# Batches on partition halves, Q and x transposed by DMA, and a new order of loads in a fused attention and MLP kernel

## The chip, the cores and the metric

The kernel runs on one core of one Trainium2 chip. The metric is the device time of one execution in microseconds (us). The kernel before takes 316.9 us (median). Times in profiles are measured from the start of the profiled execution's span, which is 1.7 to 3 us shorter than the metric. "Landing" is the time from the issue of a transfer to its arrival. TensorE is called PE, VectorE DVE, ScalarE ACT, GpSimd POOL and SyncE SP, as in the profile.

## The reference

Eight batches, eight heads, 576 tokens, 64 features a head. Attention is linear: no softmax, KV is a 64x64 matrix per head. Every output row is divided by its root mean square and multiplied by a gain, the heads are laid side by side to 4608 rows of 512, and an MLP with ELU follows.

```python
kv  = einsum('bhsd,bhse->bhde', k, v)
out = einsum('bhsd,bhde->bhse', q, kv)
out = out / sqrt(mean(out*out, -1) + 1e-6) * g_norm      # per head, 64 features
x   = out.transpose(0, 2, 1, 3).reshape(4608, 512)
h   = x @ w_in                                           # 512 -> 2048
out = where(h > 0, h, exp(min(h, 0)) - 1) @ w_out        # 2048 -> 512
```

## The kernel before

Rows are worked off in nine tiles of 512: tiles 0 to 7 are the first 512 rows of each batch, tile 8 collects the last 64 rows of all eight. While PE multiplies tile T by w_in ("first layer", eight steps of 8 products) and tile T-1 by w_out ("second layer", eight halves of 8 products), the attention of tile T+1 is slipped in between. PE needs Q and x with features on partitions, so PE itself transposes both, through PSUM (the buffers that PE's products are written to), and DVE and ACT copy the results out. The parts that matter:

```python
def q_t():                                   # Q of tile T, on PE
    qt_ps = at_tile(BF16).rearrange("p (r t) -> p r t", r=NPAIR)
    for p in range(NPAIR):
        q_t_mm(bf["q", T], qt_ps, p)         # 16 transposes in all
    nc.vector.tensor_copy(out=qT[:, 0:2, :], in_=qt_ps[:, 0:2, :])
    nc.scalar.copy(qT[:, 2:4, :], qt_ps[:, 2:4, :])
# ... cut: square, sum over a head, 1/rms by Ln and Exp, scale ...
def x_t():                                   # x of tile T, on PE: 16 more
    for c in range(KC):
        for j in range(J):
            nc.tensor.transpose(xt_ps[:, c, j*P:j*P+P], xs[:, j, c*P:c*P+P], ident)
    nc.vector.tensor_scalar(out=x[:, 0:2, :], in0=xt_ps[:, 0:2, :], scalar1=g_col, ...)
    nc.scalar.mul(x[:, 2:4, :], xt_ps[:, 2:4, :], g_col)    # the gain comes for free here
# ... cut ...
for T in range(2, NT):
    second = {i: (lambda i=i: mm2_half(T - 1, i)) for i in range(8)}
    if T + 1 < NT:
        at, start = attention(T + 1), {"kv": 0, "q": 1, "se0": 2, "se1": 4, "x": 6}
        cast_all(T + 1)                      # on POOL, fp32 to bf16
    if T + 2 < B:
        fetch(T + 2)                         # on SP's queue, in order
    first_products(T, at, second, start)
```

## Time and profile before

| | before |
|---|---|
| time, median | 316.9 us |
| first product of the first layer of tile 0 | 21.84 us |
| first product of tile 1 / tile 2 | 49.0 / 77.6 us |
| one middle tile | 31.5 us |
| last product to the end | 5.9 us |

From the page of the kernel before: busy us of each engine, its share of the span and its number of instructions, then two rows of 40 time slices, in tenths (granted PE clock; mean busy share of the 16 DMA engines).

```profile
PE 295.2 (94%) x1905; PEld 149.7 (48%) x1941; DVE 179.5 (57%) x217; ACT 155.4 (50%) x217; POOL 67.1 (21%) x117
...
PEclk9999999999999999999999999999999999999998
DMA  7999959940861076108510861034101010100122
```

PE is the bottleneck, at full clock, and from tile 2 on DMA comes in bursts, one a tile, with most of the time idle.

Busy time by stretch, kernel before: for each stretch its length, then busy us and instructions of each engine, the clock, the DMA share and the rate.

```profile
core 0: us, PE busy (x) PEld busy (x) DVE busy (x) ACT busy (x) POOL busy (x), PEclk, DMA share, GB/s
21.84:49.03 27.19, 23.30 (x178) 12.92 (x181) 18.54 (x25) 15.85 (x25) 6.41 (x11) 1.00 1.02 211
49.03:77.64 28.61, 26.93 (x187) 13.86 (x188) 18.06 (x22) 18.53 (x25) 16.58 (x28) 1.00 0.63 225
...
109.74:141.26 31.52, 31.31 (x210) 16.14 (x212) 19.48 (x22) 16.07 (x22) 8.03 (x14) 1.00 0.40 142
```

In the last line, a middle tile, PE is busy 31.3 of 31.5 us: only work taken off PE can make it shorter. The two lines above it are the filling of the pipeline, and there PE does wait.

The chain of waits, kernel before: start, length, what. It shows what the 31.5 us are made of.

```profile
109.74 1.73 PE h_ps L318 x8
111.47 1.73 PE o_ps L360 x8
113.19 1.11 PE at L165 x36
...
136.92 0.89 PE at L281 x16
...
149.39 0.89 PE at L175 x16
```

Line 318 is a step of the first layer, 360 half a product of the second, 165 the KV products, 281 the transposes of x, 175 those of Q. The last two, 0.89 us each, are what the change takes off PE.

### The profile page before, as it was taken

To read this page: it belongs to the slowest core of one execution; us is meant where nothing else is said; L and a number is where in the kernel's file an instruction comes from. 1 tells how busy PE (TensorE), PEld (TensorE's weight loads), DVE (VectorE), ACT (ScalarE), POOL (GpSimd) and SP (SyncE) were. 2 spreads that over 40 slices of the span, in tenths; PEclk is the share of its full clock that TensorE was granted. 3 is DMA by queue.
4 is the path that set the end of the run, shared out by engine and by line. 5 is a ranking of instruction groups with operands and counts; after the bars stand their busy time and mean duration, and the time that the engine had idled before them with its cause. 6 is when DMAs were issued, how large, how long until landed. Compare 5 with 4: busy or idle time off the path is not lost.

```text
span 313.9 us, 4706 instructions
## 1 busy us (share of the span) xinstructions
PE 295.2 (94%) x1905; PEld 149.7 (48%) x1941; DVE 179.5 (57%) x217; ACT 155.4 (50%) x217; POOL 67.1 (21%) x117
## 2 busy tenths in 40 slices
PE   8677979999999999999999999999999999999992
PEld 4444535444554545455545554545455445444440
DVE  4565783487267646764786468646765576544300
ACT  3555954585465445544554455445543554334210
POOL 0465205870082008200720081002000000000000
PEclk9999999999999999999999999999999999999998
DMA  7999959940861076108510861034101010100122
GB/s 254 321 290 256 206 109 388 375 149 2 264 240 67 0 265 238 69 0 278 225 67 2 261 243 67 0 112 92 69 1 67 2 67 2 67 33 34 69 67 67
DMA packets 28597, 42.24 MB, mean 135 GB/s; under 512 B 5536, under 2 KB 17824, under 8 KB 28576
## 3 DMA queue, kind: packets, MB, share of 16 engines
q1 hardware_dynamic: 24352, 37.75, 34.5%
q0 software_dynamic: 4224, 4.19, 8.0%
q8 instruction: 15, 0.25, 0.3%
q14 instruction: 6, 0.05, 0.0%
HBM read 36.70 MB, written 9.44 MB: 147 GB/s over the span
## 4 chain that ended last, share of the span: by engine, by line
PE 78%; DMA 8%; DVE 5%; ACT 3%; POOL 2%; issue 2%; SPq 1%; DVEq 0%; POOLq 0%
PE o_ps L360 36%; PE h_ps L318 34%; DMA w_in_sb<-in_moe_w_in_dram 4%; DVE gT L344 2%; DMA st_k<-in_k_dram 2%; DMA st_v<-in_v_dram 2%; PE at L165 2%; PE at L281 2%; PE at L187 2%; PE at L175 2%; ACT elu_e L327 1%; DVE elu_e L336 1%; POOL v_bf L130 1%; POOL k_bf L130 1%; DVE xs L221 1%
## 5 line engine op out<-in xcount | busy, mean ns | idle before, releaser
L318 PE MATMUL h_ps<-xT,w_in_sb 128*128 128x512 bf16 (+1 forms) x564 | 133.7, 376 | 3.6 <-DMA w_in_sb<-in_moe_w_in_dram 1.7
L360 PE MATMUL o_ps<-w_out_sb,gT 128*128 128x512 bf16 x562 | 134.4, 379 | 0.8
L327 ACT ACTIVATE elu_e<-h_ps 128x1024 bf16<-128x1024 f32 (+1 forms) x74 | 74.0, 1002 | 60.6 <-PE h_ps L318 59.4
L360 PEld LDWEIGHTS <-gT 128*128 128x128 bf16 x576 | 56.3, 98 | 67.2
L336 DVE TENSOR_SCALAR elu_e<-elu_e 128x1024 bf16<-128x1024 bf16 (+1 forms) x73 | 35.3, 484 | 91.1 <-ACT elu_e L327 90.9
L318 PEld LDWEIGHTS <-w_in_sb 128*128 128x128 bf16 x584 | 55.1, 98 | 62.9 <-DMA w_in_sb<-in_moe_w_in_dram 2.4
L344 DVE TENSOR_TENSOR gT<-elu_e,h_ps 128x1024 bf16<-128x1024 bf16 (+1 forms) x66 | 79.5, 1205 | 6.9
L130 POOL CAST q_bf<-st_q 128x512 bf16<-128x512 f32 x32 | 18.9, 628 | 132.9 <-DMA st_q<-in_q_dram 110.6
L370 ACT COPY o_sb<-o_ps 128x512 f32<-128x512 f32 x36 | 21.1, 586 | 25.4 <-PE o_ps L360 25.4
L206 ACT ACTIVATE sq<-at 128x1024 bf16<-128x1024 f32 (+1 forms) x18 | 17.5, 979 | 14.8 <-PE at L187 12.2
L130 POOL CAST v_bf<-st_v 128x512 bf16<-128x512 f32 (+1 forms) x36 | 20.9, 622 | 12.2 <-DMA st_v<-in_v_dram 11.7
L130 POOL CAST k_bf<-st_k 128x512 bf16<-128x512 f32 (+1 forms) x35 | 20.7, 636 | 7.7 <-DMA st_k<-in_k_dram 7.7
L211 DVE TENSOR_REDUCE ss<-sq 128x16 f32<-128x1024 bf16 x16 | 19.5, 1218 | 4.0 <-ACT sq L206 3.8
L221 DVE TENSOR_TENSOR xs<-at,ss 128x1024 bf16<-128x1024 f32 x16 | 19.5, 1218 | 0.6 <-ACT ss L218 0.6
L291 ACT ACTIVATE xT<-at,g_col 128x1024 bf16<-128x1024 bf16 x8 | 8.9, 1114 | 19.4 <-DVE xT L288 19.4
L421 PE MATMUL idle_ps<-zeros,ident 128*128 128x512 bf16 x43 | 12.4, 422 | 1.6 <-POOL ident masks.py:199 1.4
L250 ACT COPY qT<-at 128x1024 bf16<-128x1024 bf16 x8 | 8.1, 1012 | 11.5 <-DVE qT L249 11.5
L165 PE MATMUL at<-v_bf,k_bf 64*128 64x128 bf16 x288 | 10.1, 216 | 2.8 <-DVE v_bf L130 2.0
L165 PEld LDWEIGHTS <-k_bf 64*128 64x128 bf16 x288 | 8.4, 94 | 7.0 <-issue 5.4
L187 PEld LDWEIGHTS <-qT 128*128 128x128 bf16 x128 | 8.4, 98 | 5.9 <-issue 2.5
L187 PE MATMUL at<-bd_kv,qT 128*128 128x128 bf16 x120 | 9.1, 219 | 2.2 <-DVE xs L221 2.2
L241 ACT CAST bd_kv<-at 64x256 bf16<-64x256 f32 x14 | 5.2, 369 | 9.8 <-PE at L165 9.7
(46 smaller groups left out, 107.1 us busy)
## 6 DMA issues: line engine op xcount, KB each, us to landing
st_q<-in_q_dram SPq DMA_DIRECT2D x16, 512.0 KB, 5.5
out_dram<-o_sb SPq DMA_DIRECT2D x16, 512.0 KB, 2.6
st_k<-in_k_dram SPq DMA_DIRECT2D x7, 1152.0 KB, 8.4
st_v<-in_v_dram SPq DMA_DIRECT2D x7, 1152.0 KB, 10.8
w_in_sb<-in_moe_w_in_dram POOLq DMA_DIRECT2D x4, 512.0 KB, 18.4
w_out_sb<-in_moe_w_out_dram POOLq DMA_DIRECT2D x4, 512.0 KB, 20.0
st_k<-in_k_dram SPq DMA_DIRECT2D x2, 576.0 KB, 6.8
st_v<-in_v_dram SPq DMA_DIRECT2D x2, 576.0 KB, 7.8
```

What stands on the lines that cost most here:

```text
L130: eng.tensor_copy(out=out_, in_=in_)
L165: nc.tensor.matmul(kv_ps[s][:, u * P : u * P + P], lhsT=bf["k", T][rows, j, 2 * u : 2 * u + 2, :], rhs=bf["v", T][rows, j, 2 * u : 2 * u + ...
L187: nc.tensor.matmul(ov[:, u, :, s, :], lhsT=qT[:, p, j * P : j * P + P], rhs=bd_kv[:, T, p, :], start=True, stop=True,)
L206: nc.scalar.activation(sq, se_ps, AF.Square)
L211: nc.vector.reduce_sum(out=ss, in_=sq.rearrange("p c (h e) -> p (c h) e", h=H), axis=AX.X)
L221: nc.vector.tensor_tensor(out=xs.rearrange("p c (h e) -> p (c h) e", h=H), in0=se_ps.rearrange("p c (h e) -> p (c h) e", h=H), in1=ss.to_b ...
L318: nc.tensor.matmul(h_ps[a][:, cs], lhsT=w_in_sb[:, c, f * P : f * P + P], rhs=x[:, c, cs], start=(c == 0), stop=(c == KC - 1),)
L327: nc.scalar.activation(e[:, lo:hi, :], ps, AF.Exp)
L336: nc.vector.tensor_scalar(out=e[:, lo:hi, :], in0=e[:, lo:hi, :], scalar1=1.0, scalar2=1.0, op0=ALU.min, op1=ALU.subtract,)
L344: nc.vector.tensor_tensor(out=gT[T][:, 2 * i + lo : 2 * i + hi, :], in0=e[:, lo:hi, :], in1=h, op=ALU.add if relu else ALU.max,)
L360: nc.tensor.matmul(o_ps[T, j], lhsT=gT[T][:, f, j * P : j * P + P], rhs=w_out_sb[:, f, :], start=(f == 0), stop=(f == FC - 1),)
L370: nc.scalar.copy(o_sb[T][:, j % 2, :], o_ps.pop((T, j)))
```

## The change

The intent: (a) let DMA transpose Q and x, which frees PE of 1.78 us a tile; (b) tile by "slots" of 64 rows, so that every batch lies on partition halves and the ninth tile is no longer made of leftovers; (c) make the first two tiles with features on partitions from the start, which needs no transposed x, with the mean of squares from a product with a matrix of ones; (d) load the weights first and hold batch 1 back; (e) move all later batch loads to POOL's queue. The core of the diff, cut:

```diff
-            nc.vector.tensor_copy(out=qT[:, 0:2, :], in_=qt_ps[:, 0:2, :])      # Q through PE and PSUM
-            nc.scalar.copy(qT[:, 2:4, :], qt_ps[:, 2:4, :])
+    def turn_q(b):
+        for s in range(2):
+            nc.sync.dma_start_transpose(out=qt[:, s]..., in_=bf["q", b][s*64:s*64+64]...)
...
-        def x_t():  # 16 transposes on PE, gain applied on the way out of PSUM
+                for i in (2 * h, 2 * h + 1):                      # behind each half of x
+                    nc.sync.dma_start_transpose(
+                        out=xT[T][:, :, i * P : i * P + P], in_=st["xs"][:, i, :])
+            def gain():                                           # in place, on DVE
+                nc.vector.tensor_scalar(out=xT[T][:, :, cols], in0=xT[T][:, :, cols],
+                                        scalar1=g_col, scalar2=None, op0=ALU.mult)
...
+    def fetch_all(b):
+        for name, src in (("q", q), ("k", k), ("v", v)):
+            fetch(name, src, b, eng=nc.gpsimd)
...
+    hold(w_out_sb[0:1, 3, 0:64])            # SP waits for the first quarter of w_out
+    for name, src in (("k", k), ("v", v), ("q", q)):
+        fetch(name, src, 1)
...
+    mm2_all(0, 8)                           # then casts, KV, Q, y, mean, 1/rms, x of tile 1
...
+    early = {3: ("v",), 6: ("sum0", "inv0", "mul0"), 7: ("sum1", "inv1")}     # tile 1's window
+    late = {4: ("kv",), 5: ("se0",), 6: ("se1",), 7: ("mul1",)}
...
+            early = {2: ("sum0", "inv0"), 4: ("sum1", "inv1"), 5: ("gain0",), 7: ("gain1",)}
+            late = {0: ("kv",), 1: ("se0",), 2: ("mul0",), 3: ("se1",), 4: ("mul1", "ahead")}
+        second = {i: (lambda i=i: mm2_half(T - 1, i + 2)) for i in range(6)}
+        window(T, at, early, late, second, (), "AB")
+        mm2_half(T, 0)                      # two halves of the tile's own second layer
+        mm2_half(T, 1)
```

"early" pieces enter the engines' orders before the ELU of their step, "late" ones behind it; "ahead" is cast_all of batch T+2, then its successor's loads, then turn_q.

## The prediction

> **What bounds it now.** TensorE. The engine summary shows PE busy 295 of the 313.9 us span. Cut into stages (busy time by stretch), a middle tile takes 31.5 us with PE busy 31.3, granted clock 1.00; DVE 19.5, ACT 16.1, DMA 40%. The chain of waits spells the 31.5 out: sixteen groups of 8 products at 1.73 (27.6), KV products 1.11, Q x KV 0.89, two sets of 16 PE transposes (Q, then x) at 0.89 each. The first layer starts at 21.84 us, waits again for w_in at 27.6 and 31.4 (timeline); tile 2 starts at 78.2. The last product ends near 308, so the tail is about 6.
>
> **What the change does.**
> 1. Removes both sets of transposes from PE from tile 2 on: 1.78 us a tile, all on the critical path; seven tiles, 12.5 us. Their PSUM evacuations (DVE 0.68+0.75, ACT 1.01+1.11) go too, but hide today. Tiles that cross a batch split a few products: under 0.1 us each.
> 2. Adds per tile two DMA transposes of 64x2304 bf16 and four of 128x512 on SP, about 1.1 MB, and two gain multiplies (about 0.42 each, by the 128x1024 bf16 tensor-scalar). The Trainium skill, "DMA: Bandwidth & Descriptors", section "Latency and other measured facts", gives 261 GB/s for a non-contiguous DMA transpose: an estimate of 4 to 5 us of transfer a tile, on DMA 60% idle. No trace here has one yet. From the second half of x to its gain there are about 5 us; two transposes should land in 3 to 4.
> 3. The next output halves move behind their own tile's first layer; the last ELU (ACT 1.02, DVE 0.43+1.22, plus a gain) has about 3 us of PE work to hide behind: about 0.4 us stall. So 30.1 us a middle tile, not 29.7.
> 4. Start. Weights no longer share DMA with batch 1, and x of tile 0 is made transposed, its mean by a ones matrix. From the measured 350 GB/s and cast times the first layer starts at 17 to 18 us and w_in no longer starves it: 4 to 5 us gained. Given back in part: batch 1 loads only after the first w_out quarter, about 29 us, and lands near 35 to 42, so PE waits some 5 us before the tile-1 attention (32 output products, 6.9 us, bridge part). In tile 1's window the batch-2 attention is squeezed into steps of 1.7 us with one PSUM buffer: waits of 3 us at its second Q x KV and 3 to 4 for its transposed x. Net, tile 2 starts near 80 to 81 us with 3.5 us of tile 1's second layer done: gain 1 to 2 us.
> 5. Tail: last stores per 128 rows on two queues: about 1 us.
>
> **Sum.** 12.5 - 2.5 + 1.5 + 1: about 12 us. 316.9 becomes about 305 us; 80% range 297 to 313. Chances: faster 0.80, within 2% 0.13, slower 0.07.
>
> **What would show it.** No PE transposes after tile 1; tile period 29.7 to 30.4; first-layer start before 18.5 us; idle PE between 38 and 46 us for batch 1 or w_out; idle PE near 75 to 81 before tile 2; DMA transposes landing in 2 to 4 us.
>
> **What would make it wrong.** DMA transposes landing in over 6 us: the second gain, ahead of the last ELU in DVE's order, then stalls PE by the excess, and 2 us of it a tile cancels the gain. Or in-order SP blocking stores behind transposes. The other way, batch 1 arriving earlier gives 5 us more.

## The result

The change takes 337.4 us (median of 4 runs, 332.9 to 338.3; one of them, 338.3, counts as slow and is left out of the ratio). Executions over 1.5% slower than the fastest of the same kernel are left out of the means. Ratios here are the mean time of one kernel's runs over that of the other's of the same rounds, so not quite the ratio of the quoted medians: 1.0595, interval 1.0528 to 1.0661. It is 6% slower; I had forecast 4% faster.

| start of | before | after | note |
|---|---|---|---|
| first layer, tile 0 | 21.84 | 18.66 | predicted 17 to 18 |
| tile 1 | 49.03 | 60.84 | more of the second layer of tile 0 is done by then |
| tile 2 | 77.64 | 98.44 | predicted 80 to 81 |
| tile 3 | 109.74 | 139.19 | tile 2 took 40.75 us |
| tile 4 | 141.26 | 173.29 | tile 3 took 34.10 us |
| end of span | 313.9 | 335.6 | |

The difference of 21.7 us splits from this table. Tile 2 starts 20.8 later, but with two output halves (16 products, 3.5 us) of tile 1 already done: 17.3 net. Tile 2 adds 8.7, tile 3 adds 2.6. Tiles 4 to 8 gain 5.5 and the tail 1.4.

From the page of the change, the lines that answer to those of before:

```profile
PE 296.9 (88%) x1658; PEld 136.7 (41%) x1658; DVE 176.4 (53%) x226; ACT 144.8 (43%) x203; POOL 72.2 (22%) x134
...
PEclk9999987998958997899989999999999999999999
DMA  7999989594999599129931244237132221402222
```

PE executes 247 instructions fewer and is busy just as long: the clock row shows why, it drops in the first half of the run. The DMA row is mostly full there too, up to slice 20, and quiet afterwards.

Busy time by stretch, the change (fill to tile 1, tile 1, tile 2, tile 3, tile 5):

```profile
core 0: us, PE busy (x) PEld busy (x) DVE busy (x) ACT busy (x) POOL busy (x), PEclk, DMA share, GB/s
...
18.66:60.84 42.18, 34.67 (x190) 15.63 (x188) 21.45 (x34) 24.27 (x36) 9.53 (x12) 0.92 0.97 247
60.84:98.44 37.60, 23.77 (x140) 10.90 (x140) 18.19 (x22) 16.78 (x23) 20.84 (x41) 0.87 0.88 257
98.44:139.19 40.75, 34.78 (x185) 15.57 (x186) 19.24 (x22) 13.43 (x19) 16.95 (x33) 0.87 0.78 233
139.19:173.29 34.10, 31.58 (x182) 14.79 (x180) 19.23 (x22) 13.93 (x20) 10.79 (x21) 0.95 0.66 168
...
203.65:233.77 30.12, 29.91 (x181) 14.28 (x180) 18.60 (x22) 13.93 (x20) 0.00 (x0) 1.00 0.39 73
```

Tile 5 is the change as meant: 30.1 us, what I had predicted for every middle tile. Tiles 1, 2 and 3 are long, and the share of DMA falls from 0.88 to 0.66 as they recover.

Lines picked from the timeline, the change, in tile 1's preparation, at its end and in tile 2: start, length, engine, line, instruction, and in brackets how long the engine had been idle and what ended it.

```profile
45.71 0.62 PE L452 MATMUL qt_ps<-ident,q_bf 128*128 128x128 bf16 x7 [1.08 <-DVE q_bf L97]
48.95 0.58 PE L184 MATMUL y_ps<-qT,bd_kv 128*128 128x64 bf16 x2 [0.84 <-ACT qT L95]
50.59 1.91 PE L379 MATMUL o_ps<-w_out_sb,gT 128*128 128x512 bf16 x4
54.73 1.03 PE L379 MATMUL o_ps<-w_out_sb,gT 128*128 128x512 bf16 x4
...
81.72 0.88 PE L216 MATMUL at<-bd_kv,qT 128*128 128x128 bf16 x8 [3.75 <-DVE xs L275]
98.44 3.59 PE L358 MATMUL h_ps<-xT,w_in_sb 128*128 128x512 bf16 x8 [9.20 <-DVE xT L288]
...
115.45 9.99 SPq L282 DMA_TRANSPOSE xT<-xs  x4
115.95 0.75 POOL L87 DMA_DIRECT2D st_q<-in_q_dram  x1
116.69 0.75 POOL L87 DMA_DIRECT2D st_k<-in_k_dram  x1
117.43 0.75 POOL L87 DMA_DIRECT2D st_v<-in_v_dram  x1
129.10 0.49 DVE L288 TENSOR_SCALAR xT<-xT,g_col 128x1024 bf16<-128x1024 bf16 x1 [6.70 <-DMA xT<-xs]
130.02 1.22 DVE L335 TENSOR_TENSOR gT<-elu_e,h_ps 128x1024 bf16<-128x1024 bf16 x1
131.29 3.57 PE L358 MATMUL h_ps<-xT,w_in_sb 128*128 128x512 bf16 x8 [5.97 <-DVE gT L335]
```

Three things are to be read here, besides the waits of 3.75 and 9.20 us in tile 1's window. First, four output products take 1.91 us at 50.6 and four of the same size 1.03 at 54.7: PE runs at half clock for a while after a stretch of small waits. Second, at 115.5 SP issues the transposes of x, and half a microsecond later POOL issues the loads of a whole batch; the gain on DVE then waits 6.7 us for x, the ELU stands behind the gain on DVE, and PE waits 6.0 us for the ELU to free its PSUM. Third, after that wait 8 products take 3.57 us instead of 1.73. The Trainium skill, "TensorE: Matmul & The Clock Gate", Part 1, says that the array starts out at half clock, is released by activity and falls back after an idle window of about 3.4 us; it puts products of 512 columns at 426.7 ns cold and 215.7 ns warm. This trace agrees with the two rates (1.73 us / 8 = 216 ns warm; the 12 products of zeros at the very start take 5.30 us, about 440 ns each, although the clock column gives 1.00 there). It also shows a drop at 47.8 us with no single wait above 1.1 us; in the 3.41 us before it PE was busy for 1.48.

All x transposes of the change, and all Q transposes from batch 2 on (the view of one source line, its last line each, 282 then 307):

```profile
DMA to landing us min/median/max: 2.3/2.4/12.4
...
DMA to landing us min/median/max: 4.0/4.6/10.3
```

Alone an x transpose lands in 2.4 us, as predicted; beside loads it took up to 12.4.

### The profile page after: what moved, and what is told of

Read it like the earlier page. It is cut to its first block, busy times and chain, and to the rows that moved or that the text cites. A ratio compares the mean times of both kernels' runs of the same rounds, so it can differ in the third digit from the quotient of the medians.

```text
span 335.6 us, 4283 instructions
## 1 busy us (share of the span) xinstructions
PE 296.9 (88%) x1658; PEld 136.7 (41%) x1658; DVE 176.4 (53%) x226; ACT 144.8 (43%) x203; POOL 72.2 (22%) x134
## 3 DMA queue, kind: packets, MB, share of 16 engines
q0 software_dynamic: 9184, 25.43, 26.5%
## 4 chain that ended last, share of the span: by engine, by line
PE 68%; DVE 11%; DMA 8%; ACT 8%; issue 3%; SPq 0%; POOL 0%; DVEq 0%; POOLq 0%
PE o_ps L379 31%; PE h_ps L358 29%; DMA xT<-xs 8%; DVE gT L335 4%; ACT elu_e L318 3%; PE at L156 2%; PE idle_ps L448 2%; DVE elu_e L327 2%; PE at L216 1%; DVE xT L288 1%; ACT rT L203 1%; ACT rT L204 1%; ACT elu_h L322 1%; DVE xs L275 1%; PE qt_ps L452 1%
## 5 line engine op out<-in xcount | busy, mean ns | idle before, releaser
L358 PE MATMUL h_ps<-xT,w_in_sb 128*128 128x512 bf16 (+1 forms) x580 | 140.4, 389 | 20.9 <-DVE gT L335 10.6
L379 PE MATMUL o_ps<-w_out_sb,gT 128*128 128x512 bf16 x576 | 138.7, 387 | 1.9 <-DVE gT L335 1.2
L335 DVE TENSOR_TENSOR gT<-elu_e,h_ps 128x1024 bf16<-128x1024 bf16 (+1 forms) x68 | 82.0, 1205 | 7.1
L391 ACT COPY o_sb<-o_ps 128x512 f32<-128x512 f32 x32 | 18.7, 585 | 35.8 <-PE o_ps L379 33.0
L97 POOL CAST q_bf<-st_q 128x384 bf16<-128x384 f32 (+2 forms) x33 | 17.4, 573 | 53.8 <-DMA qT<-q_bf 32.8
L97 POOL CAST k_bf<-st_k 128x384 bf16<-128x384 f32 (+2 forms) x33 | 17.3, 568 | 16.6 <-PE at L156 13.4
L288 DVE TENSOR_SCALAR xT<-xT,g_col 128x1024 bf16<-128x1024 bf16 x14 | 7.0, 499 | 17.5 <-DMA xT<-xs 17.5
L97 POOL CAST v_bf<-st_v 128x384 bf16<-128x384 f32 (+1 forms) x31 | 15.7, 548 | 1.7 <-DMA st_v<-in_v_dram 1.7
L253 ACT ACTIVATE sq<-at 128x1024 bf16<-128x1024 f32 x14 | 14.4, 1028 | 2.3 <-PE at L216 2.2
L448 PE MATMUL idle_ps<-zeros,ident 128*128 128x512 bf16 x24 | 8.4, 506 | 1.4 <-POOL ident masks.py:199 1.4
L207 DVE SCALAR_TENSOR_TENSOR xT<-y_ps,g_col,rT 128x512 bf16<-128x512 f32 x6 | 4.5, 749 | 6.5 <-ACT rT L204 4.7
```

The lines of the kernel that those rows point to most:

```text
L97: eng.tensor_copy(out=out_, in_=in_)
L335: nc.vector.tensor_tensor(out=gT[T][:, 2 * i + lo : 2 * i + hi, :], in0=e[:, lo:hi, :], in1=h, op=ALU.add if relu else ALU.max,)
L358: nc.tensor.matmul(h_ps[a][:, cols], lhsT=w_in_sb[:, c, f * P : f * P + P], rhs=xT[T][:, c, cols], start=(c == 0), stop=(c == KC - 1 and l ...
L379: nc.tensor.matmul(o_ps[T, j], lhsT=gT[T][:, f, j * P : j * P + P], rhs=w_out_sb[:, f, :], start=(f == 0), stop=(f == FC - 1),)
L391: nc.scalar.copy(o_sb[T][:, j % 2, :], o_ps.pop((T, j)))
L448: nc.tensor.matmul(ps[:, 0, :], lhsT=ident, rhs=zeros, start=True, stop=True)
```

## The experiments

Thirteen kernels ran after the change. They are grouped by question. Tile lengths are the distances between first products of neighbouring tiles, as the chain of waits gives them (the timeline puts a product that follows a busy PE up to 0.2 us earlier).

### Do the loads slow the transposes, or does something else? (e1, e2, e5)

**e1_fetch_later**: loads of batches 4 to 7 wait for x.

```diff
+    def gated_fetch(T, b):
+        nc.gpsimd.tensor_copy(out=after_x, in_=xT[T][0:1, 3, 496:512])   # waits for transpose and gain
+        fetch_all(b)
-                    if b + 1 < B:
-                        fetch_all(b + 1)
+        gated_fetch(T + 1, T + 3)           # behind the window of tile T
```

> Edit: the loads of batches 4 to 7 are issued only after the x of the tile in hand has been transposed and scaled (GpSimd first reads a few elements of it). Theory A (the loads share the 16 DMA engines with the x transposes, which then take 7 to 12 us instead of 2.4): no x transpose lands later than about 4 us, the waits of 9.2 us before tile 2, 6.0 in tile 2 and about 3 in tile 3 shrink to under 3, 0.5 and 0.5, the slow clock after them goes too, tiles 2 and 3 fall from 40.8 and 34.1 us to about 30.2; total 337 to 312-318 us. Rival B (DMA transposes are slow when issued behind each other on the one in-order queue, whatever the loads do): landings stay at 7 to 12 us and the total stays within 4 us of 337.

Measured: 324.6 us (ratio to before 1.0256, 1.0229 to 1.0282). The slowest x transpose landed in 3.8 us. Tile 2 started at 94.5 instead of 98.4 (its wait 4.9 instead of 9.2 us) and took 35.5 us; tile 3 took 30.1. So theory A held for x and rival B fell, but the total missed the forecast's upper end by 7 us: the wait before tile 2 stayed above the 3 us that I had expected, tile 2 began at half clock after it, and the loads that had been let go now met the Q transposes of the next batch. The timeline of this run:

```profile
92.74 3.55 SPq L307 DMA_TRANSPOSE qT<-q_bf  x2
...
95.01 0.75 POOL L87 DMA_DIRECT2D st_q<-in_q_dram  x1 [0.32 <-POOL after_x L628]
...
107.93 0.35 PE L225 MATMUL at<-bd_kv,qT 128*64 128x128 bf16 x5 [2.24 <-DMA qT<-q_bf]
```

Q was issued at 92.7 and PE still waited for it at 107.9; the slowest Q transpose took 13.8 us. (In the next expectation I put PE's wait there at 7.9 us; that was ACT's wait for PE, PE itself waited 2.24.)

**e2_gain_later**: loads as in the change, the gains moved.

```diff
-            early = {2: ("sum0", "inv0"), 4: ("sum1", "inv1"), 5: ("gain0",), 7: ("gain1",)}
+            early = {2: ("sum0", "inv0"), 4: ("sum1", "inv1")}
         mm2_half(T, 0)
         mm2_half(T, 1)
+        at["gain0"]()
+        at["gain1"]()
```

> Edit: loads as in the change; only the two in-place gains move, from steps 5 and 7 of the first layer to behind the two output halves that follow it. If what costs the time is that the first gain stands ahead of the ELU in VectorE's order (theory C: order, not the transfers), the stalls in tiles 2 and 3 shrink although the x transposes still land in 7 to 12 us: tile 2 from 40.8 to about 33, tile 3 from 34.1 to about 30.5, total about 326. If the transfer itself is the limit (A), the stall only moves behind the gain to the next tile's first product, tile 2 stays above 37, total above 333. Also the 1 us stall at the end of each quiet tile should fall to under 0.5.

Measured: 326.7 us (ratio 1.0338, 1.0281 to 1.0395). The slowest x transpose still took 12.1 us, yet tile 2 fell to 33.5 us and tile 3 to 30.2, and PE waited only 0.9 us, at the next tile's first product, where it had waited 6.0:

```profile
131.52 1.90 PE L358 MATMUL h_ps<-xT,w_in_sb 128*128 128x512 bf16 x8 [0.90 <-DVE xT L288]
```

This is theory C, to the number. So the two causes are needed together in tiles 2 and 3: the loads made the transposes slow, and the place of the gain, ahead of the ELU in DVE's order, made PE pay for it. Either cure alone gives most of the loss there back. Before tile 2 the wait stayed at 8.4 us, since there the gain feeds PE directly. (My hope for the end of a tile came to nothing: quiet tiles still took 30.2.)

**e5_gate_all**: the loads wait for x and for Q, and the gains stand late.

```diff
+        nc.gpsimd.tensor_copy(out=after_x, in_=xT[T][0:1, 3, 496:512])
+        nc.gpsimd.tensor_copy(out=after_x, in_=qT[bq][0:1, 1, 1, 8, 0:16])
+        fetch_all(b)
```

> Edit: the loads of batches 4 to 7 wait for both kinds of transposes (x of the next tile and Q of the batch after), and the gains stand behind the two output halves. In the run with only the x transposes protected, those landed in 2.4 to 3.8 us but the Q transposes of batch 3 then took 13.8 us beside the loads that had been let go, and tile 2 waited 7.9 us for them. If contention is the cause for both kinds, no transpose after tile 1 lands later than 6 us, tiles 2 to 7 all take 29.6 to 30.2 us, total 312 to 316: all that the contention costs, with the fill as slow as before. If something else delays the Q transposes, tile 2 stays above 35 us and the total above 320.

Measured: 322.4 us (ratio 1.0189, 1.0144 to 1.0235, unclear), above the 312 to 316 that I expected. From the end of tile 1's window on no transpose landed later than 5.0 us, as expected; within that window the Q transposes of batch 2, which the load of batch 3 still met, took up to 10.3. By stretch (tile 1, tile 2, tile 3):

```profile
61.72:95.00 33.28, 23.78 (x141) 10.96 (x140) 17.95 (x22) 16.80 (x23) 11.64 (x22) 0.92 0.62 175
95.00:127.75 32.75, 32.56 (x185) 14.83 (x185) 19.49 (x22) 13.61 (x20) 11.09 (x23) 0.93 0.65 173
127.75:157.90 30.15, 29.96 (x180) 14.18 (x181) 18.73 (x22) 13.95 (x21) 10.93 (x23) 1.00 0.74 192
```

From tile 3 on, all is as planned. Tile 2 has no waits left but runs at a clock of 0.93, because tile 1 ends with waits of 3.7 us (second Q x KV) and 4.9 us (x). Contention and the place of the gain account for 15 us here (337.4 to 322.4); the rest of the loss lies before tile 2, and the contention inside tile 1's window is still in it.

### What does the slow clock cost, and what do transposes on PE cost? (e4, e3)

**e4_warm**: products of zeros in the waits.

```diff
+    idle(40, at_tile())                     # before tile 2
+            if i == 7 and T in (2, 3):
+                idle({2: 26, 3: 14}[T], at_tile())
```

> Edit: nothing but products of zeros, 40, 26 and 14 of them, put where TensorE waits for x before tile 2, in tile 2 and in tile 3; the waits stay, the clock should not drop. After each of these waits 8 products took 3.57 us instead of 1.73 and the next ones were partly slow, about 2.7 us a time. If the slow clock after a wait is a cost of its own, total falls by 4 to 8 us and the mean clock rises from 0.95 to 0.97-0.98; if it is not, the total stays at 337 or rises by what the added products overrun (0 to 2 us).

Measured: 332.1 us, 5.2 less than the change, with the mean clock up from 0.953 to 0.984. The waits stayed. So about 5 us of the loss was half clock after the waits, and not the waits themselves. The total alone would be thin evidence, since one of the runs of the change took 332.9 us; but that run had a mean clock of only 0.956, and the profile of e4 has the gain where the zeros are: tile 2 took 35.8 us instead of 40.75 and tile 3 32.8 instead of 34.1.

**e3_x_on_pe**: x of tiles 2 to 8 is transposed on PE again (the x_t piece of the kernel before, at step 5), Q stays on DMA.

> Edit: x of tiles 2 to 8 is transposed on TensorE again, as in the kernel before; Q stays on DMA, all else as in the change. It prices the one part. If DMA transposes of x are what the change loses by (A): quiet tiles cost 30.1 + 0.9 - up to 0.5 = 30.5 to 31.0, but tiles 2 and 3 fall to about 31 too and the wait before tile 2 from 9 to 2-3 us; total 315 to 321. If the fill of the pipeline (until the first product of tile 1 at 60.8 us) is the larger loss, it stays above 325.

Measured: 321.6 us (ratio 1.0159, 1.0141 to 1.0177), just outside the upper end of 315 to 321. A quiet tile took 30.8 us. The change without DMA transposes of x beats the change by 16 us, but not the kernel before: that points at the fill again.

### What holds the start of tile 1? (s1, s2, s3, s4)

From the first KV product of batch 1 to the first product of tile 1 the change takes 18.25 us (42.59 to 60.84). I compare that stretch.

**s1_no_hold**: the hold is removed, batch 1 loads right behind batch 0.

> Edit, on the change: batch 1 loads right behind batch 0 instead of behind the first quarter of w_out. My prediction held that TensorE would wait for the late batch 1. In the profile k, v and q of batch 1 land near 34.7, 37.7 and 40.7 us, before TensorE is through with the 32 output products at 42.6. Theory chain: what holds tile 1 is the serial chain of casts, copies, squares, means and scalings behind it, so with an early batch 1 the first product of tile 1 stays within 2 us of 60.8. Theory load: it comes 4 to 6 us earlier. Either way the first layer of tile 0 should now wait for w_in again, 1 to 5 us.

Measured: 18.2 us (46.44 to 64.62). The first layer of tile 0 now waits for w_in, so all of it lies 3.8 us later. My predicted wait for batch 1 does not exist.

**s2_no_inv**: without logarithm and exponential in tile 1 (wrong; relative error of 0.26).

```diff
+    for rt in r:
+        nc.gpsimd.memset(rt, 1.0)
     def inv_of(c, ps):
-        inv_t(r[c // 2][:, c % 2, :], ps)
+        pass
```

> Edit, on the change, wrong on purpose: the logarithm and exponential of tile 1 (8 ScalarE calls of 128x512, 0.6 to 0.7 us each) are left out, the factor is set to one. If the serial chain on ScalarE and VectorE holds tile 1 (chain), its first product comes 3 to 6 us earlier than 60.8. If TensorE's own work or the loads of w_out hold it, it moves by under 1 us.

Measured: 18.1 us (42.79 to 60.91). It is not ACT's Ln and Exp.

**s3_warm_tile1**: 17 products of zeros in PE's waits.

> Edit, on the change: 17 products of zeros in the waits of TensorE between 44.9 and 50 us, in tile 1's serial stretch, nothing else. Two theories fell here (late loads; ScalarE's logarithm and exponential). What the profile still shows between 47 and 54.5 us is TensorE nearly always busy at half clock: groups of 4 output products take 1.7 to 1.9 us instead of 0.9. If that is what holds tile 1, its first product comes at 58 to 59.5 us instead of 60.8 and the groups from 50.6 on take 0.9. If it still comes at 60.3 or later, the stretch is held by VectorE and ScalarE in a way that no single part shows, and it stays open.

Measured: 17.45 us (44.10 to 61.55). The clock was now full, the groups of four output products took 0.87 us apart, and still only 0.8 us was won (the first product came at 61.55, because this run's first layer ended later).

**s4_warm_no_inv**: both edits (wrong in the same way).

> Edit, on the change, wrong on purpose: both of the last two edits at once, zeros products in TensorE's waits and no logarithm and exponential in tile 1. From the first KV product of batch 1 to the first product of tile 1 the change took 18.25 us, without the ScalarE calls 18.1, with a warm TensorE 17.45. Theory two equal chains: each hid the other, and with both gone the stretch takes 14.5 to 16.5 us. Theory third holder (casts, copies and scalings on VectorE, or the two evacuations of the output at the end): it stays above 17 us.

Measured: 17.2 us (42.46 to 59.66). The theory of two equal chains that hide each other falls. The timeline of this run shows what is left. It is no single wait:

```profile
43.65 0.68 PE L156 MATMUL at<-v_bf,k_bf 64*128 64x128 bf16 x18 [0.52 <-DVE bd_kv L171]
...
55.14 0.38 PE L194 MATMUL y_ps<-sq,ones 128*128 128x512 bf16 x1 [0.69 <-DVE xT L207]
...
57.97 1.02 PE L379 MATMUL o_ps<-w_out_sb,gT 128*128 128x512 bf16 x4 [0.73 <-ACT o_sb L391]
59.66 1.89 PE L358 MATMUL h_ps<-xT,w_in_sb 128*128 128x512 bf16 x8 [0.67 <-ACT o_sb L391]
```

PE's own work, the hand-overs to DVE and ACT at the start (the places that the zeros fill), and two waits for evacuated output at the end. PE is busy 13.5 of the 17.2 us, about 3.7 of it with zeros (17 at 0.216), which leaves about 9.8 us of its own work. I have not taken these apart; which of them could be shortened stays open.

### What holds tile 1's window? (f1)

**f1_fill**, on e5: Q of batch 2 is turned before the stores of tile 0 enter SP's order, the load of batch 3 waits for it, POOL casts all of V, and the attention of batch 2 is spread.

```diff
-    early = {3: ("v",), 6: ("sum0", "inv0", "mul0"), 7: ("sum1", "inv1")}
-    late = {4: ("kv",), 5: ("se0",), 6: ("se1",), 7: ("mul1",)}
+    early = {3: ("sum0", "inv0"), 5: ("sum1", "inv1")}
+    late = {1: ("kv",), 2: ("se0",), 3: ("mul0",), 4: ("se1",), 5: ("mul1",)}
```

> Edit, on the change with all loads held away from transposes (322.4 us): the Q transposes of batch 2 no longer queue behind the stores of tile 0, the load of batch 3 waits for them, and the attention of batch 2 is spread over steps 1 to 5 of tile 1 instead of 4 to 7. Theory fill: what is left of the loss is that chain, so the wait of 3.7 us at its second Q x KV, the wait of 4.9 us for x and two spells of slow clock go; tile 2 starts near 84-87 us instead of 95.0 and takes 30.2 instead of 32.8; total 308 to 313. Rival: tile 1 is held by ELU work on ScalarE and VectorE or by the loads themselves; then tile 2 still starts after 91 and the total stays above 317.

Measured: 311.9 us (ratio 0.9851, 0.9807 to 0.9896), within the 308 to 313 expected. By stretch (tile 1, tile 2):

```profile
59.64:85.12 25.48, 21.78 (x140) 10.22 (x140) 17.64 (x22) 15.33 (x22) 14.61 (x24) 1.00 0.79 224
85.12:115.50 30.38, 30.19 (x184) 14.19 (x185) 19.41 (x22) 13.88 (x21) 11.45 (x23) 1.00 0.70 187
```

Tile 1 fell from 37.6 us (33.3 in e5) to 25.5, at full clock, and tile 2 to 30.4. So tile 1's window was the other large part of the loss: 10.6 us (322.4 to 311.9, from two rounds on different chips whose before runs agree within 0.2 us). The edits were made together; how much each is worth was not tried. The squeezed attention is the likeliest, because in e5 PE waited there for DVE's scaling and for x (3.75 and 4.87 us) and never for Q. But f1 also took the load of batch 3 away from the Q transposes of batch 2, which now landed in 5.6 us instead of 10.3; in e5 their second half had landed only half a microsecond before its first use, so the attention could not have been spread without that.

### How do the loads win? (e8)

**e8_packets**: each load is cut into three, by thirds of the 2,304-byte runs.

> Edit, on the change as it is: each load of a batch is cut into three, by thirds of every partition's 2,304-byte runs, so that the same bytes go in runs of 768 bytes. If the DMA engines take turns between the queues by packets, not by bytes, a transpose of small packets gets about three times the share beside such loads: the slowest x transpose lands in 4 to 7 us instead of 12.4 and the waits of 9.2, 6.0 and 3 us shrink by half or more. If they share by bytes, or the transposes wait for something else, the slowest stays above 10 us and the total near 337.

Measured: 350.1 us (two runs; ratio 1.1055, 1.0979 to 1.1131), and the slowest x transpose took 19.1 us. This run does not decide the question it was made for: the profile counts 10,336 packets on POOL's queue instead of 9,184, about 4,200 of them for weights (the kernel before, which puts nothing but weights there, has 4,224), so the packets of the loads became about 20% smaller and not three times; it has three times the issues instead, 2.2 us of POOL's time for each of q, k and v instead of 0.75. Inconclusive as to how the engines share. The Trainium skill, "DMA: Bandwidth & Descriptors", section "Queues, rings and completion order", says that each engine takes turns between queues by packets. The change has 15,232 packets under 512 B more than e3, so an x transpose is 34 small packets on each of 16 engines (15,232 / 28 / 16). That would give a load of large packets more than its turn, but no run here shows what one turn costs, nor that what the profile counts is the page's packet. Why the loads win stays open.

### One part alone: DMA transposes on the kernel before (e6, e7)

**e6_dma_only**: only Q and x of tiles 3 to 8 go through DMA, Q one tile ahead; loads stay on SP's queue at the start of each tile.

```diff
+        def q_dma():
+            for j in range(J):
+                nc.sync.dma_start_transpose(out=qT[:, :, j * P : j * P + P],
+                                            in_=bf["q", T][:, j].rearrange("p h d -> p (h d)"))
+        def x_dma(h):                       # two of 128x512 for each half of x; gain(h) as in the change
...
-        start = {"kv": 0, "q": 1, "se0": 2, "se1": 4, "x": 6}
+        start = {"kv": 0, "se0": 1, "se1": 3, "qd": 5, "gain0": 6, "gain1": 7}   # gains behind the ELU
+        # fetch(T + 2), cast_all(T + 2) and its q_dma now all in tile T
```

> Edit, on the kernel BEFORE: nothing of the new start, tiling or queues; only from tile 3 on Q and x are transposed by DMA, the Q one tile ahead, with the batch loads issued on the same in-order queue at the start of each tile, so that they are mostly done when the transposes start. If removing the transposes from TensorE is sound by itself (my prediction's first step: 1.78 us a tile) and the change loses elsewhere, six tiles fall from 31.5 to 29.7-30.2 us and the total from 316.6 to 306-311. If transposing by DMA is itself the loss, it is no faster than 316.

Measured: 317.1 us (ratio 1.0013, 0.9975 to 1.0052): nothing gained, although PE is busy 6 us less. The timeline of this run at the end of a tile:

```profile
139.82 1.22 DVE L371 TENSOR_TENSOR gT<-elu_e,h_ps 128x1024 bf16<-128x1024 bf16 x1
140.96 0.48 DVE L295 TENSOR_SCALAR xT<-xT,g_col 128x1024 bf16<-128x1024 bf16 x1
...
141.49 1.68 PE L345 MATMUL h_ps<-xT,w_in_sb 128*128 128x512 bf16 x7 [1.57 <-DVE xT L295]
```

The transposes landed in 2.4 to 5.8 us, in time. But I had put the second gain behind the last ELU on DVE, and the next tile's first product waits for that gain. The saving became a new wait.

**e7_dma_gain_first**: the same with both gains ahead of the ELUs of steps 6 and 7.

```diff
+        if "qd" in start:
+            early.setdefault(6, []).append("gain0")
+            early.setdefault(7, []).append("gain1")
```

> Edit, on the kernel BEFORE: as in the run with DMA transposes alone, which took 31.5 us a tile although TensorE did 1.8 us less, because its first product of a tile waited 1.9 us for the second gain, which I had placed behind the last ELU in VectorE's order. Here both gains stand ahead of the ELUs of steps 6 and 7. If that order was all, a middle tile takes 29.7 to 30.0 us and the total falls from 316.9 to 305-309, the size of my prediction's first step. If the transposes by DMA cost TensorE something else, the tile stays above 30.8 and the total above 312.

Measured: 306.4 us (ratio 0.9684, 0.9655 to 0.9712), correct, faster than both kernels. By stretch (tiles 2 and 3):

```profile
78.01:108.33 30.32, 30.06 (x182) 14.42 (x181) 17.61 (x22) 14.62 (x21) 7.74 (x14) 1.00 0.75 197
108.33:138.06 29.73, 29.73 (x181) 14.36 (x180) 18.78 (x23) 13.93 (x20) 7.84 (x14) 1.00 0.64 184
```

PE is busy for all of the 29.73 us. The share of DMA, 0.75 and 0.64, is as high as in tiles 2 and 3 of the change (0.78 and 0.66), and yet no x transpose landed later than 5.6 us: here the last load of a tile is issued 6 to 11 us before its first x transpose (86.8 and 92.9 us in tile 2, 111.6 and 122.7 in tile 3), not beside it. (The loads also stand on the transposes' own queue here; what that does by itself was not tried.) The whole win of the change's idea is here, with the start of the kernel before: tile 2 starts at 78.0 us.

## Why the prediction was wrong

The sum predicted about 305; measured was 337.4, so 32.4 us were missed. Against the predicted course, tile 2 started 18 us late (98.4 against 80 to 81), tile 2 took 10.6 us more than 30.1 and tile 3 took 4.0 more: 32.6. Nothing else is missing. Two steps of the prediction failed: step 4, by which tile 2 starts near 80 to 81 us (it was 98.4), and step 2, by which two transposes land in 3 to 4 us (single ones took up to 12.4 beside loads).

1. *Transposes off PE, 1.78 us a tile.* Right: PE carries no transposes after tile 1, and e7 shows the gain by itself (31.5 to 29.7 us a tile).
2. *DMA transposes land in 3 to 4 us, on DMA 60% idle.* Right for x on a quiet DMA (2.4 us; Q took 4.6 in the median, above the 2 to 4 named as a sign), wrong for tiles 1 to 3. The 60% was the figure of a middle tile of the kernel before, whose loads keep step with the tiles. In the change POOL runs ahead of PE (the load of batch 6 went out in tile 2, where the kernel before loads batch 4), so the DMA share is 0.88, 0.78 and 0.66 in tiles 1 to 3, and x took up to 12.4 us. The share alone is not the cause, since e7 did well at 0.75 and 0.64; the moment of the issue is: half a microsecond after the transposes in tile 2, and when e1 and e5 let the loads wait, x landed in 4.1 us at most. I had named this very outcome as what would make the prediction wrong, without asking when POOL would issue its loads. I also named the second gain as the one that stalls; in tile 2 it was the first. e1, e2 and e5 show the cause: 15 us with its clock cost and with what it adds to the wait before tile 2.
The rate behind the estimate (261 GB/s, from the Trainium skill, "DMA: Bandwidth & Descriptors", section "Latency and other measured facts") did not bind either: SP takes 1.24 us (median) to issue each 128x512 transpose (131 kB), which is 106 GB/s.
3. *About 0.4 us stall at a tile's end, 30.1 us.* Right in quiet tiles: 30.12 in tile 5.
4. *Start: a net gain of 1 to 2 us by tile 2.* This is the step that failed most: "tile 2 starts near 80 to 81 us" was 98.4. Its terms: the first layer began at 18.66 (predicted 17 to 18) and w_in starved it no more, but it took 16.4 us (18.66 to 35.05), not the 13.8 of its products, with waits for ELU results. Batch 1 landed when predicted, but the 5 us that PE was to wait for it did not exist (s1); the stretch of tile 1 took 18.25 us for reasons that s2, s3 and s4 spread thin and did not settle. In tile 1's window I predicted waits of 3 and of 3 to 4 us; they were 3.75 and 9.2, of which the loads caused 4.3 (9.2 to 4.9 in e5) and the late, squeezed attention, with the late Q before it, the rest (f1, edits not separated). In all, tile 2 started at 95.0 us in e5 and at 85.1 in f1; the last 4 to 5 us to the prediction lie before tile 1 or in its window, and stay open. The half clock after waits was missing from the sum: e4 puts it at 5 us.
5. *Tail: about 1 us.* 1.4 us (5.9 to 4.5).

## What to carry to other kernels

Moving work from a full engine to an idle queue is only worth its price if nothing large is issued beside it at that moment: read when each load will be issued under the order of the new kernel. A mean share does not tell it, neither the old kernel's (0.40) nor the new one's (0.66 in a slow tile, 0.64 in e7's fast one). When a transfer feeds an in-order engine, look at what stands behind its consumer in that order; the same late transfer cost 6 us ahead of the ELU and 0.9 behind it (e2), while in e6 a gain behind the ELU was the whole loss. Change one thing on the tuned kernel before rewriting its start: the one part (e7) won 3.2%, the redesign around it lost 6%, and its long waits were paid twice, by the wait and by the clock after it (e4).

## What the Trainium skill lacked or had wrong

- "Advanced Engine Details and Errata", section "X-Bar Transpose (TRN2)", says that transpose DMAs are as fast as regular ones. Lacking is what they do beside regular ones: 2.4 us alone, 12.4 us beside the load of a batch from another queue (13.8 for a Q transpose, 19.1 in e8).
- "DMA: Bandwidth & Descriptors", section "Latency and other measured facts", gives 261 GB/s for a non-contiguous transpose. The page has no issue time for transposes of these sizes: SP took 1.24 us for each 128x512 bf16 transpose and 2.06 us for each 64x2304 (medians), which bounds the former at 106 GB/s.
- "TensorE: Matmul & The Clock Gate" warns in Part 1 and in its rules of idle gaps above about 3 us, and tells of a kernel whose short idles between groups were enough, without a size. Lacking is the size: here the clock fell to half at 47.8 us with no wait above 1.1 us, after 3.41 us in which PE was busy for 1.48 (four products then took 1.91 us at 50.6 us).
- No page says that cutting a POOL-issued load into shorter runs leaves the packets nearly as large: runs of 2,304 and of 768 bytes gave 9,184 and 10,336 packets for the same 25.43 MB, weights included.
